# A shared port and measured durations in the cost model of a kernel's planner

## The chip, the cores and the metric

The kernel runs on one core of a Trainium2 chip. The core has five queues of instructions that run side by side: TensorE (PE in the profile; PEld is its weight load), VectorE (DVE), ScalarE (ACT), GpSimd (POOL) and SyncE (SP), which here issues the transfers between HBM and SBUF. Each queue runs in its own order, and semaphores make an instruction wait for instructions of other queues. An instruction that waits holds up everything behind it in its queue. The metric is the time of one execution in microseconds of the device.

## The reference

Two independent layers are computed on inputs of 2048 positions by 1024 channels in fp32, and their results stand side by side in the output of 2048 x 2048.

```python
qkv = (x @ wqkv).reshape(B, S, 3, H, Dh)        # S 2048, D 1024, H 32, Dh 32
scores = jnp.einsum("bhqd,bhkd->bhqk", q, k) * Dh ** -0.5
o = jnp.einsum("bhqk,bhkd->bhqd", softmax(scores), v)
a = o.reshape(B, S, D) @ wo                     # attention, all positions

re = jnp.einsum("bsd,ed->bse", xb, dft_hid_re)
im = jnp.einsum("bsd,ed->bse", xb, dft_hid_im)
b = jnp.einsum("ts,bse->bte", dft_seq_re, re) - jnp.einsum("ts,bse->bte", dft_seq_im, im)
out = jnp.concatenate([a, b], axis=-1)
```

## The kernel before

The dense products (the projection to q, k and v; the two DFTs; the output projection) are done by one level of a seven-product scheme in place of eight block products (`STEPS` and `ORDER` list the seven). Each block product takes a sum or difference of input blocks, and each such operand is split into a high part and a low remainder, both of type fp32r; three matmuls (high by high, low by high, high by low) replace one of full precision. So a 256 KB block, 128 partitions by 512 columns, goes through these steps:

- a load, issued by SP (L380, a second term L389);
- an addition or subtraction of a second block, `raw<-raw,g` (L396), when the scheme asks for it;
- a cast to the high part `h` (L418 on VectorE, L416 on ScalarE when the planner may choose);
- a subtraction for the low part `l` (L421).

L396 and L421, and a few other additions, are instructions with two inputs in SBUF. The planner may give each of them to GpSimd, with a price of `SUB`, or to VectorE, with a price of `ADD`. Tiles with names such as `slot`, `raw`, `er`, `h` and `l` are these operands. Results come out of PSUM by an evacuation on VectorE (L564, L566, L768, L770, L781).

Attention runs per head. Scores S = QK are computed by TensorE into 128 x 1024 tiles of PSUM (L1069), VectorE takes the negative row maximum of each (`negm`, L1075), and ScalarE computes the exponential with row sums (L1078). A second pass computes the scores transposed (T, L1201), with the row maxima as two more rows of the contraction; ScalarE takes their exponential into `pt` (L1205), and TensorE multiplies `pt` with the values in groups of sixteen products (V, L1219). VectorE adds each group to the head's output (L1230, L1232), and the head is scaled by the reciprocal sums (L1247).

The order of the work is not that of the loops. The loops only register operations with the class `Plan`, each with an engine, a cost in microseconds, what it waits for, a rank, and for some a second engine with its own cost and rank. At the end one main loop simulates the machine with these costs. Whenever an engine is free in this simulation, the operation with the lowest rank among those that are able to start is emitted, and its end is computed. TensorE gets the scores, the transposed scores and the value products of the heads in turn, and dense matmuls of the seven-product scheme ("fills") are placed between them at a pace that keeps both streams in proportion. What the simulation decides becomes the fixed order of all five queues. At run time semaphores keep the data right; the times are the machine's own.

The costs stand in `Plan` (`LAT`, `OVERLAP`, `SLACK`, `KB_US`, `LANDING`, `QUEUE`) and in the kernel's body (`MM` for a matmul, `PV` and `SWITCH` for a group of value products, `ES` and `ET` for the two exponentials, `MAX`, `EVAC`, `CAST`, `BIT`, `SUB`, `ADD`). A transfer ends at its place in a bandwidth of `KB_US` KB per us plus `LANDING`; `SLACK` is added before a consumer of a transfer counts as able to start, so that the queues don't run into a transfer that is late. SP may run ahead of the modelled bandwidth by `QUEUE`.

This is the heart of the plan before:

```python
    def start(self, o, e=None):
        e = e or o.engine
        o.emit(e) if o.other else o.emit()
        o.begun = True
        self.free[e] = self.now + (o.cost if e == o.engine else o.other[1])
...
                if not able or self.begin(e) > self.now:
                    break
                self.start(heapq.heappop(able)[3], e)
```

Of the kernel before, what the change touches and what calls it, by code (L numbers as in the profile page):

```python
# [34 lines left out]
class Op:  # L35


    __slots__ = ("engine", "cost", "emit", "rank", "kb", "other", "left", "ready", "end", "begun", "then", "soon", "lanes")

    def __init__(self, engine, cost, emit, rank=0.0, kb=0, other=None):  # L40
        self.engine, self.cost, self.emit, self.rank, self.kb, self.other = engine, cost, emit, rank, kb, other
        self.left, self.ready, self.end, self.begun, self.lanes = 0, -1e3, None, False, 1
        self.then, self.soon = [], []


class Ring:
# [14 lines left out]
class Plan:  # L61
# [22 lines left out]
    def op(self, engine, cost, emit, after=(), uses=(), rank=0.0, kb=0, order=None, other=None, lanes=1):  # L84

        o = Op(engine, cost, emit, rank, kb, other)
        o.lanes = lanes
        seen = set()  # L90
        for d in after:
            if d is not None and id(d) not in seen:
                seen.add(id(d))
                self._wait(o, d)
        for u in uses:
            u.append(o)
        if order is not None:
            p, order.first = order.first, o
            if p is not None and not p.begun:
                p.soon.append(o)  # L100
                o.left += 1
        if o.left == 0:
            self._release(o)
        return o
# [18 lines left out]
    def start(self, o, e=None):  # L123
        e = e or o.engine
        o.emit(e) if o.other else o.emit()
        o.begun = True
        self.free[e] = self.now + (o.cost if e == o.engine else o.other[1])
        if o.kb:
            for _ in range(o.lanes):
                t = max(self.free[e], self.lane[0])  # L130
                self.dma = max(self.dma, t) + o.kb / o.lanes / self.KB_US
                o.end = self.dma + self.LANDING
                self.lane = self.lane[1:] + [o.end]
                if o.lanes > 1:
                    self.free[e] = t + o.cost
        else:
            o.end = self.free[e]
            self.free[e] -= self.OVERLAP.get(e, 0.0)
        for t in o.then:
            t.ready = max(t.ready, self.after(o, e, t))  # L140
            t.left -= 1
            if t.left == 0:
                self._release(t)
        for t in o.soon:
            t.ready = max(t.ready, self.now)
            t.left -= 1
            if t.left == 0:
                self._release(t)
        o.then = o.soon = ()
        o.emit = None  # L150

    def others(self):

        for e, pend in self.pending.items():
            able = self.able[e]
            while True:
                while pend and pend[0][0] <= self.now:
                    t, s, r, o = heapq.heappop(pend)
                    heapq.heappush(able, (r, t, s, o))
                while able and able[0][3].begun:  # L160
                    heapq.heappop(able)
                if not able or self.begin(e) > self.now:
                    break
                self.start(heapq.heappop(able)[3], e)

    def next_time(self):
        t = 1e18
        for e, pend in self.pending.items():
            able = self.able[e]
            while able and able[0][3].begun:  # L170
                heapq.heappop(able)
            while pend and pend[0][3].begun:
                heapq.heappop(pend)
            if able:
                t = min(t, self.begin(e))
            elif pend:
                t = min(t, max(self.begin(e), pend[0][0]))
        return t
# [7 lines left out]
def kernel(  # L186
# [101 lines left out]
    ACAST = 0.6  # L288
# [12 lines left out]
    op = pl.op  # L301
# [56 lines left out]
    def fetch(shape, terms, store=None, keep=None):  # L358

        box = {}  # L360
        raws, seconds, tile_of, gate = where[0]
        rank = seq()
        sign, *first = terms[0]
        loaded = len(first) == 2
        if len(terms) == 1 and not loaded:
            return first[0].get, first[0].made, first[0].users
        if keep is None:
            old, users = raws.take()
        else:
# [12 lines left out]
        for sign, *term in terms[1:]:  # L382
            other = {}
            if len(term) == 2:
                gold, gusers = seconds.take()

                def load(src=term[0], other=other):
                    other["q"] = tile_of(shape, "g", len(seconds.users))
                    nc.sync.dma_start(other["q"], src)  # L389

                q = op("SP", ISSUE, load, gold + term[1] + gate, [gusers], rank, 256, seconds)
            else:
                other["k"], q, gusers = term[0], term[0].made, term[0].users

            def add(e, sign=sign, other=other, a=None if last is not None else first[0]):
                (nc.gpsimd if e == "POOL" else nc.vector).tensor_tensor(  # L396
                    out=dest(), in0=dest() if a is None else a.get(), in1=other["q"] if "q" in other else other["k"].get(), op=ALU.add if sign > 0 else ALU.subtract)

            last = op("POOL", SUB, add, old + [first[0].made if last is None else last, q], [users, gusers] + ([first[0].users] if last is None else []),
                      rank, 0, raws if keep is None and last is None else None, other=("DVE", ADD, 20 + rank))  # L400
            old = []
        if keep is not None:
            keep.made = last
        if store is not None:
            store[1].append(op("SP", ISSUE, lambda: nc.sync.dma_start(store[0], dest()), [last], [users], rank, 256))
        return dest, last, users

    spare = [True]

    def halves(raw, made, users, hi, lo, old, mine, order=(None, None)):  # L410

        rank = seq()
# [7 lines left out]
        def low(e):  # L420
            (nc.gpsimd if e == "POOL" else nc.vector).tensor_tensor(out=lo(), in0=raw(), in1=f(hi()), op=ALU.subtract)  # L421

        a = op("DVE", CAST, high, [made] + old[0], [users, mine[0]], 10 + rank, 0, order[0], ("ACT", ACAST, 25 + rank) if spare[0] else None)
        b = op("POOL", SUB, low, [a] + old[1], [users, mine[0], mine[1]], rank, 0, order[1], other=("DVE", ADD, 25 + rank))
        return a, b

    def piece(terms, store=None):
# [316 lines left out]


    def add_op(emit, after, users, rank):
        return op("POOL", SUB, emit, after, users, rank, other=("DVE", ADD, 20 + rank))

    def gather(what, X, Y, u3, to, wrote, part=None):

# [293 lines left out]
    def scores(h):  # L1044
# [79 lines left out]
    mine = {}  # L1124
    rt = {}

    def sums(h):
# [262 lines left out]
```

## Time and profile before

| what | value |
|---|---|
| median of 3 runs | 3123.39 us (3119.55 to 3124.46) |
| profiled execution, its own time | 3121.61 us |
| profiled execution, span from first to last instruction | 3119.8 us |
| mean granted clock of TensorE | 0.994 |
| TensorE busy | 98% of the span |
| VectorE busy | 80% |
| ScalarE busy | 74% |
| GpSimd busy | 30% |
| moved between HBM and SBUF | 567.77 MB, mean 182 GB/s |

The profile is one execution. A row of a group of instructions names the line, the engine, the operation, what it writes and reads (output <- inputs) and the shapes; then follow the count, the busy time and the mean duration of one in ns, and the idle time of the engine just before them with what ended it. In a timeline a row gives start, duration, engine, line, operation, and in brackets the idle time before it with its releaser. A wait is a triple: total us, times, longest us. Ends of matmuls are modelled, so a matmul's shown duration of about 400 ns overlaps the next one.

### The profile page before, as it was taken

What the parts mean: (1) busy time and instruction counts of PE and PEld (TensorE: products, weight loads), DVE (VectorE), ACT (ScalarE), POOL (GpSimd) and SP (SyncE); (2) the same over time, 40 slices, a digit from 0 to 9 for tenths busy, and PEclk for the clock granted to TensorE, in tenths of its full rate; (3) what the DMA queues carried; (4) which work ended last, traced back from release to release, by engine and by line L of the source; (5) the groups of instructions that cost most, each with busy time, mean ns of one, the idle gap of its engine ahead of it and who ended that gap; (6) DMA issues with size and microseconds to landing.
All of it is one profiled execution on the core that took longest, in us unless ns stands there. A gap on an engine that the chain in (4) does not pass through costs nothing.

```text
span 3119.8 us, 45400 instructions
## 1 busy us (share of the span) xinstructions
PE 3066.8 (98%) x15040; PEld 2151.0 (69%) x15040; DVE 2503.5 (80%) x3182; ACT 2299.1 (74%) x4316; POOL 924.9 (30%) x683
## 2 busy tenths in 40 slices
PE   9899999899999999999999999999999999999999
PEld 7687666566666666666676666666666666666787
DVE  6669888878777878887777798888877888887886
ACT  4237888778888888888888878888888887775321
POOL 3423323412112321122111253323211244433443
PEclk9999999999999999999999999999999999999999
DMA  9975557876634544464433576445433467546952
GB/s 333 326 241 192 184 159 246 291 233 217 182 86 145 190 132 155 135 189 147 133 126 104 180 241 195 146 148 173 141 115 98 141 213 232 159 150 206 330 172 91
DMA packets 359673, 567.77 MB, mean 182 GB/s; under 512 B 86640, under 2 KB 88176, under 8 KB 359440
## 3 DMA queue, kind: packets, MB, share of 16 engines
q1 hardware_dynamic: 359440, 564.87, 56.8%
q8 instruction: 121, 1.98, 0.3%
q14 instruction: 112, 0.92, 0.1%
HBM read 407.70 MB, written 156.50 MB: 181 GB/s over the span
## 4 chain that ended last, share of the span: by engine, by line
PE 66%; DVE 6%; ACT 1%; issue 1%; DMA 0%; POOL 0%; SPq 0%; ACTq 0%; DVEq 0%; POOLq 0%
PE pd L332 29%; PE psT L1201 12%; PE pd L1219 11%; PE psS L1069 11%; PE psT L332 3%; DVE negm L1075 2%; ACT psS L1078 1%; DVE raw L396 1%; DVE h L418 1%; DVE slot L421 1%; DVE l L421 0%; DVE slot L770 0%; DVE slot L418 0%; DVE e L781 0%; PE psS L1152 0%
## 5 line engine op out<-in xcount | busy, mean ns | idle before, releaser
L1075 DVE TENSOR_REDUCE negm<-psS 128x1 f32<-128x1024 f32 x1024 | 1231.9, 1217 | 206.2 <-PE psS L1069 202.4
L1205 ACT ACTIVATE pt<-psT 128x512 f32<-128x512 f32 x2048 | 1155.4, 627 | 322.0 <-PE psT L1201 315.7
L1078 ACT ACTIVATE psS<-psS,negm 128x1024 f32<-128x1024 f32 x1024 | 1146.6, 1120 | 187.0 <-DVE negm L1075 179.9
L332 PE MATMUL pd<-slot,h 128*128 128x512 f32 x3336 | 1157.8, 397 | 3.2 <-DVE ot L1232 1.7
L1201 PE MATMUL psT<-qs,ks 98*128 98x512 f32 x2048 | 822.4, 405 | 5.1 <-ACT pt L1205 4.2
L332 PEld LDWEIGHTS pd<-slot,h 128*128 128x128 f32 x3336 | 632.4, 190 | 156.9 <-issue 12.6
L332 PE MATMUL pd<-slot,l 128*128 128x512 f32 x1668 | 661.5, 397 | 0.8 <-POOL l L421 0.8
L1201 PEld LDWEIGHTS psT<-qs,ks 98*128 98x128 f32 x2048 | 385.9, 189 | 193.2 <-issue 65.6
L1069 PE MATMUL psS<-ks,qs 96*128 96x512 f32 x1552 | 479.0, 399 | 12.1 <-ACT psS L1078 11.1
L1219 PE MATMUL pd<-pt,vt 128*32 128x512 f32 x4096 | 470.9, 601 | 4.5 <-DVE c L564 2.6
L421 POOL TENSOR_TENSOR l<-raw,h 128x512 fp32r<-128x512 f32 x174 | 233.1, 1339 | 798.5 <-DVE h L418 407.7
L396 POOL TENSOR_TENSOR raw<-raw,g 128x512 f32<-128x512 f32 x229 | 307.9, 1348 | 422.6 <-DVE raw L396 102.4
L332 PEld LDWEIGHTS pd<-slot,l 128*128 128x128 f32 x1668 | 316.7, 190 | 76.0 <-issue 5.7
L1069 PEld LDWEIGHTS psS<-ks,qs 96*128 96x128 f32 x1552 | 289.3, 189 | 95.2 <-ACT psS L1078 30.4
L1219 PEld LDWEIGHTS pd<-pt,vt 128*32 128x32 f32 x4096 | 121.2, 110 | 283.6 <-issue 262.1
L421 POOL TENSOR_TENSOR slot<-raw,slot 128x512 fp32r<-128x512 f32 x131 | 182.2, 1396 | 396.6 <-DVE slot L418 319.0
L1078 ACT ACTIVATION_READ_ACCUMULATOR psS<-psS,negm 128x1 f32 x1024 | 242.0, 236 | 0.0
L332 PE MATMUL pd<-slot,slot 128*128 128x512 f32 x768 | 195.9, 393 | 0.0
L1232 DVE TENSOR_TENSOR ot<-ot,pd 128x512 f32<-128x512 f32 x96 | 65.8, 686 | 134.6 <-PE pd L1219 134.5
L332 PEld LDWEIGHTS pd<-slot,slot 128*128 128x128 f32 x768 | 145.0, 189 | 32.2 <-issue 0.4
L418 DVE CAST h<-raw 128x512 fp32r<-128x512 f32 x305 | 153.4, 503 | 15.8 <-PE pd L332 13.8
L421 DVE TENSOR_TENSOR slot<-raw,slot 128x512 fp32r<-128x512 f32 x153 | 156.4, 1025 | 6.0 <-ACT slot L416 2.4
(114 smaller groups left out, 2093.5 us busy)
## 6 DMA issues: line engine op xcount, KB each, us to landing
raw<-in_ct SPq DMA_DIRECT2D x224, 256.0 KB, 3.4
g<-in_ct SPq DMA_DIRECT2D x128, 256.0 KB, 3.5
c<-u_d SPq DMA_DIRECT2D x104, 256.0 KB, 3.6
qk_d<-e SPq DMA_DIRECT2D x52, 512.0 KB, 3.8
qs<-qk_d SPq DMA_DIRECT2D x128, 192.0 KB, 3.7
ks<-qk_d SPq DMA_DIRECT2D x128, 192.0 KB, 2.7
raw<-ab_d SPq DMA_DIRECT2D x96, 256.0 KB, 2.9
g<-ab_d SPq DMA_DIRECT2D x80, 256.0 KB, 3.6
```

The source lines that it names most:

```text
L332: nc.tensor.matmul(box["ps"], a[1]((a[0].hi, a[0].lo)[u]()), b[1]((b[0].hi, b[0].lo)[v]()), start=k == 0, stop=k == n - 1)
L396: (nc.gpsimd if e == "POOL" else nc.vector).tensor_tensor(out=dest(), in0=dest() if a is None else a.get(), in1=other["q"] if "q" in other ...
L418: nc.vector.tensor_copy(hi(), raw())
L421: (nc.gpsimd if e == "POOL" else nc.vector).tensor_tensor(out=lo(), in0=raw(), in1=f(hi()), op=ALU.subtract)
L1069: nc.tensor.matmul(p[:, i * NB : i * NB + NB], (qx["t"] if own else QS[h % 2][0:96])[:, qt * P : qt * P + P], KS[h % 2][0:96, c * 1024 + i ...
L1075: nc.vector.tensor_reduce(out=ST["negm"][:, c, qt : qt + 1], in_=box["p"], axis=AX.X, op=ALU.max, negate=True)
L1078: nc.scalar.activation(box["p"], box["p"], AF.Exp, bias=ST["negm"][:, c, qt : qt + 1], accum_out=ST["sums"][:, c, qt : qt + 1])
L1201: nc.tensor.matmul(box["p"], KS[h % 2][0:98, t * P : t * P + P], QS[h % 2][0:98, j * NB : j * NB + NB], start=True, stop=True)
L1205: nc.scalar.activation(box["t"], box["p"], AF.Exp)
L1219: nc.tensor.matmul(po["p"][j * DH : j * DH + DH, :], VT[h][:, k, :], box["t"], start=(k == t + 1 - PVB), stop=(k == t), tile_position=(0, ...
L1232: nc.vector.tensor_tensor(out=po["o"], in0=po["o"], in1=po["p"], op=ALU.add)
```

## The change

The planner's simulation gets a resource that two engines use. An operation can be marked `two`: a VectorE operation that is taken to use the port that VectorE shares with GpSimd. Marked are the casts (L418), all additions and subtractions that may go to GpSimd or VectorE (L396, L421, L786, L1019, L1247), and the small operations of a head's maxima and sums with inputs in SBUF (L1099, L1137, L1146). Every GpSimd operation counts as a user. While the port is taken in the simulation, GpSimd starts nothing, and VectorE starts the lowest-ranked operation that is not marked, if there is one.

```diff
+        self.port = 0.0
...
         self.free[e] = self.now + (o.cost if e == o.engine else o.other[1])
+        if e == "POOL" or e == "DVE" and o.two:
+            self.port = self.free[e]
...
-                self.start(heapq.heappop(able)[3], e)
+                o = self.choose(e, able)
+                if o is None:
+                    break
+                self.start(o, e)
+
+    def choose(self, e, able):
+        if self.port <= self.now or e not in ("DVE", "POOL"):
+            return heapq.heappop(able)[3]
+        if e == "POOL":
+            return None
+        for x in sorted(able):
+            if not x[3].two and not x[3].begun:
+                able.remove(x)
+                heapq.heapify(able)
+                return x[3]
+        return None
```

The function that finds the next moment of the simulation takes the port into account in the same way. The other part of the change is the numbers. Durations of single operations are replaced, and the model of transfers is changed:

```diff
-    SLACK = {("SP", "POOL"): 2.0, ("SP", "DVE"): 2.5, ("SP", "PE"): 2.0, ("POOL", "DVE"): 0.7}
-    KB_US = 340.0
-    LANDING = 1.8
+    SLACK = {("SP", "POOL"): 2.0, ("SP", "DVE"): 2.0, ("SP", "PE"): 2.0, ("POOL", "DVE"): 0.7}
+    KB_US = 380.0
+    LANDING = 1.6
...
-    MM, PV, SWITCH, TINY = 0.232, 0.87, 0.34, 0.25
-    ES, ET = 1.22, 0.61
-    MAX, EVAC, CAST, BIT = 1.22, 0.69, 0.45, 0.27
-    SUB = 1.34
+    MM, PV, SWITCH, TINY = 0.234, 0.762, 0.62, 0.25
+    ES, ET = 1.235, 0.625
+    MAX, EVAC, CAST, BIT = 1.22, 0.685, 0.415, 0.275
+    SUB = 1.31
...
-    ADD = 0.69
+    ADD = 0.68
...
-        a = op("DVE", BIT, nmin, maxes + nold, [nuse, suse], -2)
+        a = op("DVE", 0.17, nmin, maxes + nold, [nuse, suse], -2, two=True)
...
-        a = op("DVE", 2 * BIT, sub, exps + told, [tuse, suse, nuse], -2)
+        a = op("DVE", 0.24, sub, exps + told, [tuse, suse, nuse], -2, two=True)
...
-        c = op("DVE", 3 * BIT, inv, [b], [tuse, suse], -2)
+        c = op("DVE", 0.67, inv, [b], [tuse, suse], -2, two=True)
```

The set of operations and transfers stays the same. What can change is the order in each of the five queues, and the choice of engine for an operation that has two.

More of the change, by code (lines that the diff above doesn't have):

```diff
@@ L35, with __init__ @@
 class Op:
-    __slots__ = ("engine", "cost", "emit", "rank", "kb", "other", "left", "ready", "end", "begun", "then", "soon", "lanes")
-    def __init__(self, engine, cost, emit, rank=0.0, kb=0, other=None):
+    __slots__ = ("engine", "cost", "emit", "rank", "kb", "other", "left", "ready", "end", "begun", "then", "soon", "lanes", "two")
+    def __init__(self, engine, cost, emit, rank=0.0, kb=0, other=None, two=False):
         self.engine, self.cost, self.emit, self.rank, self.kb, self.other = engine, cost, emit, rank, kb, other
@@ L43, in __init__ @@
         self.then, self.soon = [], []
+        self.two = two
 class Ring:
@@ L80, in __init__, with op @@
         self.dma = 0.0
+        self.port = 0.0
         self.lane = [0.0] * 8
         self.seq = 0
-    def op(self, engine, cost, emit, after=(), uses=(), rank=0.0, kb=0, order=None, other=None, lanes=1):
-        o = Op(engine, cost, emit, rank, kb, other)
+    def op(self, engine, cost, emit, after=(), uses=(), rank=0.0, kb=0, order=None, other=None, lanes=1, two=False):
+        o = Op(engine, cost, emit, rank, kb, other, two)
         o.lanes = lanes
@@ L174, in next_time @@
             if able:
-                t = min(t, self.begin(e))
+                u = self.begin(e)
+                if e == "POOL" or e == "DVE" and all(x[3].two or x[3].begun for x in able):
+                    u = max(u, self.port)
+                    if pend:
+                        u = min(u, max(self.begin(e), pend[0][0]))
+                t = min(t, u)
             elif pend:
@@ L399, in fetch @@
             last = op("POOL", SUB, add, old + [first[0].made if last is None else last, q], [users, gusers] + ([first[0].users] if last is None else []),
-                      rank, 0, raws if keep is None and last is None else None, other=("DVE", ADD, 20 + rank))
+                      rank, 0, raws if keep is None and last is None else None, other=("DVE", ADD, 20 + rank), two=True)
             old = []
@@ L421, in low @@
             (nc.gpsimd if e == "POOL" else nc.vector).tensor_tensor(out=lo(), in0=raw(), in1=f(hi()), op=ALU.subtract)
-        a = op("DVE", CAST, high, [made] + old[0], [users, mine[0]], 10 + rank, 0, order[0], ("ACT", ACAST, 25 + rank) if spare[0] else None)
-        b = op("POOL", SUB, low, [a] + old[1], [users, mine[0], mine[1]], rank, 0, order[1], other=("DVE", ADD, 25 + rank))
+        a = op("DVE", CAST, high, [made] + old[0], [users, mine[0]], 10 + rank, 0, order[0], ("ACT", ACAST, 25 + rank) if spare[0] else None, two=True)
+        b = op("POOL", SUB, low, [a] + old[1], [users, mine[0], mine[1]], rank, 0, order[1], other=("DVE", ADD, 25 + rank), two=True)
         return a, b
@@ L746, in add_op @@
     def add_op(emit, after, users, rank):
-        return op("POOL", SUB, emit, after, users, rank, other=("DVE", ADD, 20 + rank))
+        return op("POOL", SUB, emit, after, users, rank, other=("DVE", ADD, 20 + rank), two=True)
     def gather(what, X, Y, u3, to, wrote, part=None):
```

## The prediction

> **What bounds the kernel now.** I read the busy table first, then the busy times by stage, then the chain of waits, then single stalls in order of time, and last the groups of instructions for the prices. The busy table:
>
> ```profile
> PE 3066.8 (98%) x15040; PEld 2151.0 (69%) x15040; DVE 2503.5 (80%) x3182; ACT 2299.1 (74%) x4316; POOL 924.9 (30%) x683
> ```
>
> TensorE is the bound on average: of 3119.8 us of span it lacks 53 us. A plan that only reorders work can win those 53 us and what the clock loses after them, no more. Where they lie is told by five stages (columns: stretch, its length, then busy time and count of PE, PEld, DVE, ACT, POOL; then granted clock, DMA share, GB/s):
>
> ```profile
> 0.00:156.00 156.00, 138.92 (x575) 112.70 (x576) 103.74 (x130) 57.62 (x96) 60.78 (x48) 0.96 0.98 330
> 156.00:468.00 312.00, 307.87 (x1468) 224.91 (x1470) 255.87 (x332) 216.40 (x398) 94.85 (x70) 1.00 0.61 194
> 468.00:702.00 234.00, 221.34 (x1068) 144.06 (x1061) 194.48 (x258) 177.99 (x335) 71.68 (x54) 0.96 0.79 257
> 702.00:2886.00 2184.00, 2171.39 (x10942) 1485.80 (x10941) 1762.06 (x2239) 1795.06 (x3404) 600.88 (x449) 1.00 0.51 160
> 2886.00:3120.00 234.00, 227.27 (x1000) 183.57 (x998) 187.32 (x226) 52.03 (x85) 96.73 (x63) 0.99 0.58 198
> ```
>
> TensorE's idle time is 17.1 us in the first stage (the DMA engines are full there, 0.98), 4.1 in the second, 12.7 in the third, 12.6 in the fourth and 6.7 in the last. The third stage is the densest after the start, and the clock shows there too: 0.96 over 234 us is 0.08 of it, 19 us, at half speed. One stall of that stage in order of time:
>
> ```profile
> 603.45 3.07 POOL L421 TENSOR_TENSOR slot<-raw,slot 128x512 fp32r<-128x512 f32 x2 [0.36 <-DVE slot L418]
> 603.63 1.78 DVE L421 TENSOR_TENSOR l<-raw,h 128x512 fp32r<-128x512 f32 x1
> 605.33 1.21 DVE L1075 TENSOR_REDUCE negm<-psS 128x1 f32<-128x1024 f32 x1
> 606.63 1.09 ACT L1078 ACTIVATE psS<-psS,negm 128x1024 f32<-128x1024 f32 x1 [2.64 <-DVE negm L1075]
> 608.38 0.50 PE L1201 MATMUL psT<-qs,ks 98*128 98x512 f32 x1 [3.55 <-ACT pt L1205]
> 608.79 0.41 DVE L418 CAST e<-e 128x512 fp32r<-128x512 f32 x1
> 609.24 0.69 DVE L421 TENSOR_TENSOR e<-e 128x512 fp32r<-128x512 f32 x1
> ```
>
> Read it upward from 608.38: TensorE idled 3.55 us for ScalarE's exponential, which had idled 2.64 us for VectorE's maximum, which stood behind a subtraction of 1.78 us. The same operation takes 0.69 us at 609.24. The difference ends with GpSimd's first operation, which had started 0.18 us before it: VectorE waited for GpSimd while holding up its whole queue. The same pattern stands in the fourth stage on the chain of work that ended last (start, duration, what):
>
> ```profile
> 2583.30 1.41 DVE h L418
> 2584.74 1.67 DVE l L421
> 2586.40 1.15 DVE negm L1075
> ```
>
> Over the part of the run that the chain covers (797 us to the end), these lines of VectorE hold 0.5, 0.5, 0.5 and 0.4% of the span, 59 us:
>
> ```profile
> by line: PE pd L332 29.0%; PE psT L1201 11.8%; PE pd L1219 11.1%; PE psS L1069 10.9%; PE psT L332 2.8%; DVE negm L1075 2.2%; ACT psS L1078 0.8%; issue 0.6%; DVE raw L396 0.5%; DVE h L418 0.5%; DVE slot L421 0.5%; DVE l L421 0.4%; DVE slot L
> ```
>
> **The change part by part.** *The port in the plan.* The program runs every queue in the order that the planner wrote, so the planner's false beliefs become real stalls. It believed that a cast takes 0.45 us and a subtraction 0.69 us at any moment. The groups say otherwise (count | busy, mean ns | idle before):
>
> ```profile
> L421 DVE TENSOR_TENSOR slot<-raw,slot 128x512 fp32r<-128x512 f32 x153 | 156.4, 1025 | 6.0 <-ACT slot L416 2.4
> L421 DVE TENSOR_TENSOR l<-raw,h 128x512 fp32r<-128x512 f32 x147 | 117.3, 798 | 5.0 <-ACT h L416 0.7
> L396 DVE TENSOR_TENSOR raw<-raw,g 128x512 f32<-128x512 f32 x143 | 113.1, 799 | 8.0 <-DMA raw<-t_d 2.4 <-POOL raw L396 1.5 <-DMA raw<-in_xb 1.2
> L418 DVE CAST h<-raw 128x512 fp32r<-128x512 f32 x305 | 153.4, 503 | 15.8 <-PE pd L332 13.8 <-POOL l L421 1.2 <-issue 0.3
> L418 DVE CAST slot<-raw 128x512 fp32r<-128x512 f32 x233 | 126.1, 547 | 1.8 <-DMA raw<-ab_d 1.0 <-POOL slot L421 0.2
> ```
>
> Against 0.69 and 0.41 us undisturbed, the excess is 153 x 0.335 + 147 x 0.108 + 143 x 0.109 + 305 x 0.093 + 233 x 0.137 = 51 + 16 + 16 + 28 + 32 = 143 us of VectorE. After the change such an operation is not placed while GpSimd works; a maximum or an evacuation out of PSUM is placed instead, and GpSimd's next operation waits for VectorE's. So 143 us bounds what VectorE can get back, and TensorE sees only what lies on its path. There the 59 us of the chain set the bounds: at the groups' mean (0.33 of a 1025 ns operation is excess, 0.14 of one of 798) 8 to 19 us are excess; if all were like the 1.67 us one, 0.59 of them, 35 us.
>
> *Operations that change engine.* In the built programs GpSimd has 63 tensor operations fewer (688 to 625), VectorE 56 more and ScalarE 7 more; TensorE's 12,928 matmuls (the profile records each attention-value product twice, hence 15,040) and the 2,345 entries of SP's queue keep their number and kinds. VectorE takes on 56 x 0.69 = 39 us; this is covered by the idle 20% of VectorE (616 us) and by the excess that goes. In the third stage VectorE is 194 of 234 us busy and this cover is thin: the longest-loaded part of it has these rows (same columns as the stages):
>
> ```profile
> 536.00:562.00 26.00, 23.27 (x100) 14.99 (x97) 23.03 (x28) 20.14 (x37) 13.99 (x11) 0.87 0.93 323
> 580.00:600.00 20.00, 16.55 (x86) 10.19 (x85) 19.90 (x31) 12.45 (x24) 8.23 (x6) 1.00 0.92 310
> 600.00:612.00 12.00, 8.40 (x38) 4.21 (x40) 9.89 (x13) 7.74 (x14) 4.42 (x3) 0.88 1.00 336
> ```
>
> VectorE is busy without a gap from 580 to 600, with the DMA engines at 0.92. There I expect less to be won than the collisions are worth: what goes first is itself waiting.
>
> *Durations of single operations.* The matmul goes from 0.232 to 0.234, the maximum stays at 1.22, the exponentials become 1.235 and 0.625, a group of sixteen attention-value products goes from 0.34 + 4 x 0.87 = 3.82 to 0.62 + 4 x 0.762 = 3.67 us. A row of the chain agrees with the new value for the group, 3.57 us:
>
> ```profile
> 2512.77 3.57 PE pd L1219 x32
> ```
>
> In the built program the mix is hardly moved: 945 dense matmuls follow the last attention group instead of 953, and 273 precede the first score instead of 281. I price this at nothing for TensorE's work, with 2 us either way for the order in which kinds of matmul follow each other.
>
> *Transfers believed faster and the slack cut.* A 256 KB load for a VectorE operation was taken to be safe 0.46 + 256/340 + 1.8 + 0.1 + 2.5 = 5.6 us after its issue with an idle queue; it becomes 0.46 + 256/380 + 1.6 + 0.1 + 2.0 = 4.8. Here the trace bounds from both sides (median us from issue to landing; the first two from 702 to 2886 us, the next from 540 to 640, the last two from the first 156):
>
> ```profile
> raw<-in_ct SPq DMA_DIRECT2D x206, 256.0 KB, 3.3
> raw<-ab_d SPq DMA_DIRECT2D x96, 256.0 KB, 2.9
> ...
> raw<-in_wqk SPq DMA_DIRECT2D x11, 256.0 KB, 4.9
> ...
> er<-in_xa SPq DMA_DIRECT2D x40, 256.0 KB, 5.3
> raw<-in_xa SPq DMA_DIRECT2D x28, 256.0 KB, 5.6
> ```
>
> In the long fourth stage 4.8 leaves 1.5 us and more of margin, so the cut costs nothing there and may let operands be ready up to 0.8 us earlier. In the third the margin is gone at the median, unless the planner's own queue model, which adds up to 1 us, covers it. What waits behind a late load is all of VectorE's queue, the maxima first, and behind them ScalarE and the scores. I take +3 us for the third stage (two to four waits of about 1 us that reach TensorE), with 0 and 13 as ends, the latter from the rival below. The first stage is bound by bytes at 330 GB/s, which do not change: 0, within 3 either way.
>
> *The sum.* Second stage 4.1 idle: half of it goes, -2. Third stage: 12.7 idle and about 8 more for 19 us at half clock, together some 21; half, -10, plus 3 for late loads. Fourth: 12.6 idle; two thirds, -8, because its loads have margin and VectorE has room. Last stage: about 4 of its 6.7 are the last store, the rest holds one more collision of the same kind: -1.5. First: 0. Together -18.5, and with 1.5 for order -17. The profiled execution took 3121.6 us, so 3104.6; the median of the runs shown is 1.8 higher, so I forecast 3106.
>
> *A rule weighed.* At 603.45 the row shows VectorE's subtraction ending about when GpSimd's operation does, so the port was held for a whole operation. The Trainium skill, SBUF — State Buffer, section "Who interferes with whom", says just that: the pair is locked exclusively for a full instruction, the later one blocks entirely, and which of them suffers is decided by the order of issue alone. The trace agrees (1.78 against 0.69 us). The page therefore speaks against a large gain: a lock that is held can be planned around, but not shortened, and two queues with no semaphore between them still take it in whatever order they arrive. By it the result would be that of the second rival below.
>
> **The rivals.** *Late loads at the head of VectorE's queue (slower).* Place: the stages with full DMA engines. GpSimd absorbed most late loads; VectorE has few such waits (us in sum, times, longest):
>
> ```profile
> POOL l L421 <- DVE h L418: 409.8, 92, 22.7
> ...
> POOL raw L396 <- DMA raw<-in_ct: 49.6, 18, 5.5
> POOL raw L396 <- DMA raw<-in_xb: 47.6, 10, 9.5
> ...
> DVE er L396 <- DMA raw<-in_xa: 12.7, 8, 2.9
> ```
>
> With 0.8 us less slack and more of the adds on VectorE, waits move there. If 80 of the 981 operations of the five groups came 0.8 us late, VectorE would wait 64 us; TensorE lost about 30 us in the middle stages against 143 us of excess, one in five, so +13 us. And a plan whose loads are late no longer keeps GpSimd and VectorE apart, so nothing is won: 3123 + 13 = 3136. It decides when about one in twelve of these operations waits so. For it: 4.9 to 5.6 us to landing in two stages. Against: 3.3 us in the stage that is 70% of the run.
>
> *The order of two queues holds no lock (no change).* The plan only chooses an order for each engine; nothing makes GpSimd start at the planned moment. If the real times drift by more than half of a 1.3 us operation, the collisions fall at other places in like number. For it: landings of equal loads differ between 2.9 and 5.6 us. Against: GpSimd's longest waits in sum end with VectorE's own cast (92 waits above), not with a load, so drift is shared. The gain would be a quarter, 3119.
>
> *All of it goes.* The four middle stages lose two thirds to all of their idle time, the half-clock stretches go with it, and the earlier readiness in the fourth stage adds: 32 idle + 8, less 3: 3086. For it: nearly every stall that I followed in stages two to four has an inflated VectorE operation in front of it. Against: VectorE at 100% from 580 to 600 us.
>
> **How the numbers follow.** Forecast 0.55, its own range 3095 to 3115; no change 0.17; slower 0.14; all of it 0.14. Outside 0.2% (6 us, about what a measurement of this kernel can tell) lie the forecast almost whole and the third rival: faster 0.69. Within: the second rival and a little of the forecast, 0.18. Slower: the first, 0.13. The range reaches to 3088, which leaves out most of the third rival's lower half, and to 3130, which leaves out most of the first; together no more than 2 in 10.
>
> **What the new profile would show.** Right: the means of the five groups above fall towards 690 and 415 ns (1025 to under 850, 547 to under 480); VectorE's lines L396, L418, L421 hold under 1.3% of the chain, not 1.9; TensorE's idle time falls from 53 to about 38 us, most in 468 to 702 and 702 to 2886, with a clock of 0.98 or more in the third stage; the first stage stays at 17. Wrong by the first rival: new waits of VectorE for loads, above 30 us in sum. Wrong by the second: means unchanged. What I could have missed is a change of the work's order that starves ScalarE of scores; it would show as idle TensorE in the fourth stage before the scores, with the groups' means down all the same.

## The result

The changed kernel takes 3089.56 us (median of 4 runs, 3087.53 to 3091.51) against 3122.46 us before (4 runs); the ratio is 0.9895, with a 95% interval of 0.9878 to 0.9912. That is 33 us less; the forecast was 17 us less, 3106 with a range down to 3088. The profiled execution took 3091.5 us with a span of 3089.7.

The busy table of the changed kernel (its code lines have numbers higher by 25, so L396, L418, L421, L1075 and L1078 are now L421, L443, L446, L1100 and L1103):

```profile
PE 3052.6 (99%) x15040; PEld 2154.2 (70%) x15040; DVE 2432.0 (79%) x3238; ACT 2312.0 (75%) x4323; POOL 828.8 (27%) x620
```

TensorE's idle time fell from 53.0 to 37.1 us, and its busy time fell too, by 14.2 us, with the same 15,040 records. To see where, the two executions have to be cut at the same amount of TensorE's work. First the changed kernel, cut where the start of its 575th, 2043rd, 3111th and 14,053rd record lies (columns as in the prediction: stretch, length, PE, PEld, DVE, ACT, POOL, clock, DMA share, GB/s):

```profile
0.00:157.30 157.30, 139.84 (x575) 112.05 (x576) 103.76 (x145) 60.01 (x98) 41.78 (x35) 0.95 0.98 338
157.30:467.60 310.30, 308.46 (x1470) 227.58 (x1468) 245.01 (x331) 216.30 (x397) 95.70 (x72) 1.00 0.61 192
467.60:688.70 221.10, 215.62 (x1071) 143.50 (x1070) 185.78 (x251) 179.70 (x339) 80.13 (x60) 0.98 0.82 270
688.70:2862.20 2173.50, 2165.34 (x10943) 1490.93 (x10942) 1720.38 (x2275) 1803.14 (x3402) 549.12 (x412) 1.00 0.51 161
2862.20:3089.70 227.50, 223.28 (x989) 180.16 (x987) 177.06 (x240) 52.88 (x91) 62.08 (x41) 1.00 0.57 198
```

Then the kernel before, cut at the same records:

```profile
0.00:155.90 155.90, 138.82 (x574) 112.64 (x575) 103.64 (x130) 57.62 (x96) 60.78 (x48) 0.96 0.98 330
155.90:468.40 312.50, 308.37 (x1472) 225.07 (x1475) 256.37 (x333) 216.80 (x399) 94.85 (x70) 1.00 0.61 194
468.40:704.10 235.70, 223.04 (x1073) 145.66 (x1066) 196.18 (x259) 179.48 (x337) 72.39 (x54) 0.96 0.80 257
704.10:2888.50 2184.40, 2171.78 (x10943) 1486.16 (x10942) 1760.65 (x2239) 1793.78 (x3402) 600.18 (x448) 1.00 0.51 160
2888.50:3119.80 231.30, 224.77 (x989) 181.50 (x987) 186.63 (x225) 51.44 (x84) 96.73 (x63) 0.99 0.58 197
```

The same work takes +1.4, -2.2, -14.6, -10.9 and -3.8 us, in sum the 30.1 us by which the spans differ. In this pair of plans nearly half comes from the third stage, in which VectorE and the DMA engines are both densely loaded. The nudged kernels below show that this stage moves by up to 12 us with any new order, and that the fourth stage gains in every pair.

The groups of VectorE that the prediction used, in the changed kernel (count | busy, mean ns | idle before):

```profile
L443 DVE CAST h<-raw 128x512 fp32r<-128x512 f32 x305 | 138.6, 455 | 20.0 <-PE pd L357 17.0 <-DMA raw<-in_xb 1.1 <-issue 1.0
L446 DVE TENSOR_TENSOR l<-raw,h 128x512 fp32r<-128x512 f32 x176 | 131.8, 751 | 5.8 <-ACT h L441 2.1
L443 DVE CAST slot<-raw 128x512 fp32r<-128x512 f32 x230 | 115.0, 504 | 3.9 <-DMA raw<-in_wd 3.2
L421 DVE TENSOR_TENSOR raw<-raw,g 128x512 f32<-128x512 f32 x148 | 114.7, 783 | 8.4 <-DMA raw<-t_d 3.0 <-DMA raw<-in_ct 1.5 <-DMA g<-ab_d 1.1
L446 DVE TENSOR_TENSOR slot<-raw,slot 128x512 fp32r<-128x512 f32 x142 | 105.4, 747 | 5.5 <-ACT slot L441 3.1
```

With the prediction's undisturbed durations (0.69 and 0.41 us) the excess is 305 x 0.045 + 176 x 0.061 + 230 x 0.094 + 148 x 0.093 + 142 x 0.057 = 14 + 11 + 22 + 14 + 8 = 69 us, where it was 143. By this measure half of the collisions' cost is gone, not all.

One wait of ScalarE stands between such a collision and TensorE: the exponential of a score tile that waits for its maximum (total us, times, longest). Before:

```profile
ACT psS L1078 <- DVE negm L1075: 179.9, 167, 8.3
```

After:

```profile
ACT psS L1103 <- DVE negm L1100: 111.9, 122, 8.7
```

This wait fell with the time here, but it does not set the time alone: one kernel below (transfers alone) has 148.6 us of it and the time of before, another (without GpSimd) has 110.1 us and is 16 us slower than the changed one. The chain of waits in the fourth stage moved as well. Before (the chain reaches back to 796 us), maxima held 3.2% of the time and the casts, additions and subtractions another 2.6%:

```profile
by line: PE pd L332 36.8%; PE psT L1201 16.9%; PE pd L1219 15.7%; PE psS L1069 15.6%; DVE negm L1075 3.2%; ACT psS L1078 1.2%; DVE h L418 0.8%; issue 0.7%; DVE l L421 0.6%; DVE slot L418 0.4%; DVE slot L421 0.4%; DVE raw L396 0.4%; PE psS L
```

After, maxima hold half of that share, and of the others only `h` and `raw` stand in the part of the line that is shown:

```profile
by line: PE pd L357 40.2%; PE psT L1226 18.5%; PE pd L1244 17.4%; PE psS L1094 16.9%; DVE negm L1100 1.6%; ACT psS L1103 0.6%; issue 0.6%; PE psS L1177 0.4%; PE psS L1128 0.4%; DVE h L443 0.4%; DVE raw L421 0.3%; DMA g<-ab_d 0.3%; POOL raw 
```

### The profile page after: what moved, and what is told of

Same layout as the page of the kernel before. It is cut to its first block, busy times and chain, and to the rows that moved or that the text cites. A ratio compares the mean times of both kernels' runs of the same rounds, so it can differ in the third digit from the quotient of the medians.

```text
span 3089.7 us, 45419 instructions
## 1 busy us (share of the span) xinstructions
PE 3052.6 (99%) x15040; PEld 2154.2 (70%) x15040; DVE 2432.0 (79%) x3238; ACT 2312.0 (75%) x4323; POOL 828.8 (27%) x620
## 4 chain that ended last, share of the span: by engine, by line
PE 90%; DVE 4%; DMA 4%; issue 1%; ACT 1%; SPq 1%; POOL 0%; POOLq 0%; ACTq 0%; DVEq 0%
PE pd L357 39%; PE psT L1226 15%; PE psS L1094 15%; PE pd L1244 15%; PE psT L357 6%; DVE negm L1100 1%; DMA er<-in_xa 1%; ACT psS L1103 1%; DMA raw<-in_wqk 0%; DMA raw<-in_wv 0%; DMA qk_d<-e 0%; DVE raw L421 0%; DMA raw<-in_xa 0%; DVE h L443 0%; PE psS L1177 0%
## 5 line engine op out<-in xcount | busy, mean ns | idle before, releaser
L1100 DVE TENSOR_REDUCE negm<-psS 128x1 f32<-128x1024 f32 x1024 | 1234.8, 1220 | 224.6 <-PE psS L1094 220.0
L1103 ACT ACTIVATE psS<-psS,negm 128x1024 f32<-128x1024 f32 x1024 | 1139.5, 1113 | 122.2 <-DVE negm L1100 111.9
L446 POOL TENSOR_TENSOR l<-raw,h 128x512 fp32r<-128x512 f32 x145 | 194.3, 1340 | 876.5 <-DVE h L443 374.0
L421 POOL TENSOR_TENSOR raw<-raw,g 128x512 f32<-128x512 f32 x224 | 294.7, 1322 | 483.9 <-DVE raw L421 75.6
L446 POOL TENSOR_TENSOR slot<-raw,slot 128x512 fp32r<-128x512 f32 x142 | 198.8, 1405 | 492.8 <-DVE slot L443 334.4
L1103 ACT ACTIVATION_READ_ACCUMULATOR psS<-psS,negm 128x1 f32 x1024 | 234.5, 229 | 0.0
L443 DVE CAST h<-raw 128x512 fp32r<-128x512 f32 x305 | 138.6, 455 | 20.0 <-PE pd L357 17.0
L1094 PE MATMUL psS<-ks,qx 96*128 96x512 f32 x496 | 151.2, 397 | 1.7 <-ACT psS L1103 1.4
```

The lines of the kernel that those rows point to most:

```text
L443: nc.vector.tensor_copy(hi(), raw())
L1094: nc.tensor.matmul(p[:, i * NB : i * NB + NB], (qx["t"] if own else QS[h % 2][0:96])[:, qt * P : qt * P + P], KS[h % 2][0:96, c * 1024 + i ...
L1100: nc.vector.tensor_reduce(out=ST["negm"][:, c, qt : qt + 1], in_=box["p"], axis=AX.X, op=ALU.max, negate=True)
L1103: nc.scalar.activation(box["p"], box["p"], AF.Exp, bias=ST["negm"][:, c, qt : qt + 1], accum_out=ST["sums"][:, c, qt : qt + 1])
```

## The experiments

The change has three parts: the port in the plan, the durations, the transfer numbers. My theory was that the port carries the gain. The rivals were the corrected numbers, and the luck of a new order: a planner like this turns any small change into another order of five queues.

**The port alone, and the numbers alone.** The first kernel is the changed one with the numbers of before, the second the kernel before with all numbers of the change.

```diff
 # port alone: the changed kernel, and
-    SLACK = {..., ("SP", "DVE"): 2.0, ...};  KB_US = 380.0;  LANDING = 1.6
+    SLACK = {..., ("SP", "DVE"): 2.5, ...};  KB_US = 340.0;  LANDING = 1.8
-    MM, PV, SWITCH, TINY = 0.234, 0.762, 0.62, 0.25
+    MM, PV, SWITCH, TINY = 0.232, 0.87, 0.34, 0.25
 # and so on for every duration; numbers alone is the reverse, on the kernel before
```

> The port in the plan, with every duration and transfer number of before. My theory (the gain of 33 us comes from keeping VectorE's two-port operations and GpSimd apart): most of it, 3095 to 3107 us, the groups slot<-raw,slot and l<-raw,h at 700 to 800 ns on VectorE as in the changed kernel. Rival (the corrected durations and transfer numbers carry it): 3112 to 3124. Rival (any new order of the plan moves the time as much): anything from 3080 to 3140.

> All the numbers of the change (durations and transfers), without the port. My theory: 3110 to 3122 us, the means of the VectorE groups unchanged from before (1025, 798, 799, 503, 547 ns). Rival (the numbers carry it): 3089 to 3100.

The port alone: 3086.67 us, ratio 0.9886 (0.9872 to 0.9901). The numbers alone: 3143.14 us, ratio 1.0067 (1.0051 to 1.0082). So the port carries the whole gain, more than I expected of it, and the numbers without it make the kernel slower by 20.5 us, which neither expectation had foreseen. The stages of the kernel with the numbers alone, cut at the same records, show where:

```profile
151.40:473.10 321.70, 313.36 (x1471) 226.21 (x1473) 266.89 (x342) 218.92 (x401) 90.48 (x66) 0.99 0.60 189
473.10:701.50 228.40, 217.51 (x1071) 141.97 (x1072) 199.02 (x263) 181.20 (x343) 64.34 (x48) 0.99 0.81 262
701.50:2899.70 2198.20, 2176.48 (x10944) 1484.90 (x10943) 1793.99 (x2297) 1802.74 (x3396) 529.71 (x392) 1.00 0.51 159
2899.70:3142.80 243.10, 229.44 (x989) 183.02 (x987) 186.11 (x225) 50.73 (x83) 93.69 (x61) 0.98 0.54 185
```

Against the kernel before, +9 us in the second stage, -7 in the third, +14 in the fourth and +12 in the last. Its collisions are as many as before (two of the five groups):

```profile
L421 DVE TENSOR_TENSOR l<-raw,h 128x512 fp32r<-128x512 f32 x184 | 155.1, 843 | 9.8 <-ACT h L416 4.8
L421 DVE TENSOR_TENSOR slot<-raw,slot 128x512 fp32r<-128x512 f32 x151 | 150.9, 1004 | 6.9 <-ACT slot L416 3.2
```

The excess of these two is 184 x 0.153 + 151 x 0.314 = 76 us, against 67 for the same two before. Corrected durations of undisturbed operations don't tell a plan of collisions.

**Is it the luck of an order?** `LATE` is a margin that TensorE's operations get in the plan; it stands for nothing that was measured. Moved by 3%, it gives all queues a new order.

```diff
-    LATE = 0.3
+    LATE = 0.31
```

> The kernel before with one constant of the planner that stands for nothing measured moved by 3% (LATE from 0.30 to 0.31), which gives the queues a new order. My theory: within 6 us of before, 3117 to 3128. Rival (any new order moves the time as much as the change did): more than 12 us away.

> The changed kernel with the same constant moved by 3% (LATE from 0.30 to 0.31). My theory: within 6 us of the changed kernel, 3084 to 3096. Rival (the 33 us are the luck of one order): closer to the kernel before than to the changed one, above 3105.

> The port with the numbers of before, and LATE at 0.31. The nudge moved the kernel before by 10 us and the changed kernel by 13, so a single pair tells no more than some 12 us. If the port carries the gain in any order: 3082 to 3105, at least 20 us under the nudged kernel before (3133). If port_alone was the luck of one order: above 3110.

> The numbers without the port, and LATE at 0.31. If the numbers without the port truly cost 20 us: 3135 to 3150. If the 3143 of the first try were the spread of orders: 3115 to 3135. Either way at least 20 us above the nudged changed kernel (3103), if the port carries the gain.

Medians in us, with the ratio to the kernel before in brackets where it was not given yet:

| | no port, LATE 0.30 | no port, LATE 0.31 | port, LATE 0.30 | port, LATE 0.31 |
|---|---|---|---|---|
| numbers of before | 3122.46 | 3132.87 (1.0023 to 1.0046) | 3086.67 | 3096.93 (0.9907 to 0.9937) |
| numbers of the change | 3143.14 | 3162.81 (1.0119 to 1.0149) | 3089.56 | 3102.66 (0.9923 to 0.9953) |

I had expected the nudge to stay within 6 us; it costs 10 to 20 us in each of the four pairs, so a difference of that size between two single plans tells nothing of its cause. The nudged kernel with the new numbers alone lies above both ranges that I had set for it. The port is outside of that spread: -36, -36, -54 and -60 us in the four pairs. The new numbers cost 21 and 30 us without the port, and 3 and 6 us with it, which is inside the spread. So in these plans the numbers did harm only to a planner that didn't know the port.

The same traces tell which stage the port shortens. Lengths in us, cut at the same records as above:

| | no port, LATE 0.30 | no port, LATE 0.31 | port, LATE 0.30 | port, LATE 0.31 |
|---|---|---|---|---|
| third stage, numbers of before | 235.7 | 245.5 | 221.9 | 233.8 |
| third stage, numbers of the change | 228.4 | 237.0 | 221.1 | 223.7 |
| fourth stage, numbers of before | 2184.4 | 2184.0 | 2172.6 | 2162.9 |
| fourth stage, numbers of the change | 2198.2 | 2208.8 | 2173.5 | 2179.1 |

The rows of the fourth stage in the four nudged kernels, in the order before, port alone, numbers alone, changed:

```profile
717.80:2901.80 2184.00, 2171.78 (x10947) 1486.04 (x10943) 1766.92 (x2267) 1795.05 (x3388) 575.80 (x431) 1.00 0.51 161
699.70:2862.60 2162.90, 2162.37 (x10950) 1493.03 (x10942) 1706.73 (x2271) 1790.33 (x3384) 571.23 (x423) 1.00 0.52 162
707.00:2915.80 2208.80, 2182.28 (x10950) 1494.25 (x10946) 1792.75 (x2296) 1799.59 (x3388) 555.08 (x409) 1.00 0.52 159
686.20:2865.30 2179.10, 2169.39 (x10944) 1495.41 (x10943) 1750.07 (x2312) 1794.41 (x3388) 535.53 (x398) 1.00 0.52 162
```

In the fourth stage every plan with the port is shorter than every plan without it, by 12 to 30 us in the pairs. In the third the pairs give 7 to 14 us, but the nudge alone moves it by 3 to 12, and the two kinds of plan overlap.

**Which of the numbers.**

```diff
 # transfers alone, on the kernel before
-    SLACK = {..., ("SP", "DVE"): 2.5, ...};  KB_US = 340.0;  LANDING = 1.8
+    SLACK = {..., ("SP", "DVE"): 2.0, ...};  KB_US = 380.0;  LANDING = 1.6
 # durations alone, on the kernel before
-    MAX, EVAC, CAST, BIT = 1.22, 0.69, 0.45, 0.27
+    MAX, EVAC, CAST, BIT = 1.22, 0.685, 0.415, 0.275
 # and all other durations of the change
```

> The kernel before with the three transfer numbers alone (KB_US 380, LANDING 1.6, slack of VectorE behind a load 2.0). If the late loads of my first rival cost what the numbers alone lost (20 us): 3135 to 3150, with VectorE's waits for loads above 40 us. If the durations cost it: 3115 to 3133, within what a nudge of the plan does.

> The kernel before with the corrected durations alone. If they cost what the numbers alone lost (a shorter belief of a cast and a subtraction packs VectorE's port work closer, so that collisions grow): 3133 to 3150, the groups slot<-raw,slot and raw<-raw,g above 1000 and 840 ns. If the transfers cost it: 3110 to 3133.

Transfers alone: 3119.83 us, ratio 0.9997 (0.9988 to 1.0007). Durations alone: 3129.17 us, ratio 1.0028 (1.0019 to 1.0037). With the transfers alone VectorE's waits for loads do rise, from 24 us to 52 us, which is the sign that I had named, but the time stays; so late loads are not what the numbers lost. The wait for the maxima is shorter than before, without a gain:

```profile
ACT psS L1078 <- DVE negm L1075: 148.6, 140, 6.2
```

The durations cost 9 us, as much as a nudge does, and of the two means that I had named one grew past its mark (1041 ns) and the other didn't (828 ns). The two parts together lost 20.5 us. The 11 us between that and the sum of the parts are of the size of a nudge, and what caused them stays open.

**What of the port brings it.** In the changed plan two things happen while GpSimd holds the port: VectorE's marked operations wait, and others go first. This kernel was meant to keep the first and take the second away (the function that finds the next moment is changed to match):

```diff
-        for x in sorted(able):
-            if not x[3].two and not x[3].begun:
-                able.remove(x)
-                heapq.heapify(able)
-                return x[3]
-        return None
+        return None if able[0][3].two else heapq.heappop(able)[3]
```

> The changed kernel, but while the port is taken VectorE waits with its first-ranked operation in the plan instead of letting an unmarked one go first. Theory A (the gain comes from the maxima and evacuations that go first): most of the gain is gone, 3108 to 3125. Theory B (the gain comes from a plan that knows how long VectorE really takes): it stays, 3086 to 3100. In both the groups' means stay at 740 to 790 ns.

3112.05 us, ratio 0.9968 (0.9956 to 0.9979): 22 us of the 33 are gone, in the range of theory A. The collisions are about as rare as in the changed kernel:

```profile
L438 DVE CAST h<-raw 128x512 fp32r<-128x512 f32 x305 | 143.8, 472 | 23.4 <-PE pd L352 17.8 <-DMA raw<-in_ct 1.9 <-DMA r_d<-rs 1.3
L441 DVE TENSOR_TENSOR slot<-raw,slot 128x512 fp32r<-128x512 f32 x149 | 111.3, 755 | 8.2 <-ACT slot L436 5.4
```

and the exponentials wait longer for the maxima, 139.9 us against 111.9:

```profile
ACT psS L1098 <- DVE negm L1095: 139.9, 147, 8.0
```

But the edit takes away less than theory A needs, so it can't decide between the two. In both kernels the planner starts the lowest rank first, and maxima and evacuations have the ranks 0 and -1, while casts, additions and subtractions have 10 and more. So a maximum that becomes able to start while GpSimd holds the port goes ahead of a waiting cast in this kernel too. What the edit takes away is the overtaking of a head's small marked operations (L1099, L1137 and L1146 before), which have rank -2. In the plan of the changed kernel an unmarked operation overtakes a marked one 31 times, each time one of these and never a cast, an addition or a subtraction.

So this run prices something narrower: the small operations hold up VectorE's queue in the plan while they wait for GpSimd. It cost 22 us on one pair of plans, where the nudge moves the kernels with the port by 10 and 13. Of the 22 us, 11.5 lie in the third stage (232.6 against 221.1), the one that moves with any new order; the fourth takes 2178.2 us, still within the four plans with the port above. Whether the port's gain comes from the maxima that go ahead or from a plan that knows how long VectorE takes stays open: no run gives VectorE true durations without letting the maxima pass.

**No GpSimd at all.** The change also takes 63 operations off GpSimd. This kernel takes off all of them:

```diff
-            heapq.heappush(self.pending[o.engine], (o.ready, self.seq, o.rank, o))
+            if o.engine != "POOL":
+                heapq.heappush(self.pending[o.engine], (o.ready, self.seq, o.rank, o))
```

> The changed kernel, but no addition or subtraction goes to GpSimd: all 620 run on VectorE at 0.69 us, so no collision is left. VectorE would be busy 2432 + 620 x 0.69 less about 70 of excess, 2790 us or 90%. My theory (GpSimd is worth having, if it is kept apart): 3100 to 3140. Rival (what the change won is only the work taken off GpSimd): at most 3090. The five groups' means fall to 690 and 410 to 420 ns in both.

3105.24 us, ratio 0.9949 (0.9934 to 0.9964). GpSimd keeps 8 small operations of 4.3 us, the collisions are gone, and VectorE has the clean durations on which the sums above rest:

```profile
PE 3065.5 (99%) x15040; PEld 2160.8 (70%) x15040; DVE 2658.4 (86%) x3856; ACT 2306.9 (74%) x4317; POOL 4.3 (0%) x8
...
L447 DVE TENSOR_TENSOR slot<-raw,slot 128x512 fp32r<-128x512 f32 x284 | 192.0, 686 | 4.6 <-ACT slot L442 3.2
L444 DVE CAST slot<-raw 128x512 fp32r<-128x512 f32 x233 | 96.5, 420 | 4.6 <-DMA raw<-ab_d 2.6 <-DMA raw<-in_wv 1.0 <-DMA raw<-in_xa 0.2
```

That is 16 us under the kernel before, which is inside what a nudge can move. The closer comparison has the same numbers in its plan: the kernel with the numbers alone takes 3143.14 us, 38 us more, and the same with the nudge 58 more. (The port is still in this kernel's plan. There it acts on VectorE alone, which passes its own marked operations in the 0.08 us by which the plan lets two of VectorE's operations overlap.) So with these numbers and a plan that was blind to the port, GpSimd's work cost more than it gave; with the numbers of before this is not shown. Against the changed kernel the stages are these (cut at the same records, the third to the last):

```profile
463.30:703.70 240.40, 226.82 (x1072) 145.23 (x1065) 216.08 (x321) 187.97 (x354) 0.00 (x0) 0.96 0.77 248
703.70:2876.20 2172.50, 2167.79 (x10944) 1495.55 (x10943) 1888.73 (x2687) 1790.66 (x3382) 0.00 (x0) 1.00 0.51 162
2876.20:3104.00 227.80, 223.16 (x989) 180.25 (x987) 170.83 (x283) 52.34 (x88) 0.00 (x0) 1.00 0.56 198
```

The third stage, where VectorE is now 90% busy, is longer than in each of the four plans with the port (240.4 us against 221.1 to 233.8); the fourth is within their spread (2172.5 against 2162.9 to 2179.1). The whole is 16 us slower than the changed kernel, but only 3 us slower than the changed kernel with the nudge, so what a GpSimd kept apart is worth is shown for the third stage at most. I had expected VectorE at 2790 us and it has 2658: the durations of its records add up to 2894 us (2584 in the changed kernel), but neighbouring records overlap, and the busy time counts an overlap once.

**Can the rest be had?** Two attempts on the port alone: hold the port 0.15 us longer in the plan, and let GpSimd start nothing while a marked operation of VectorE's own, which is a cast or a small one of a head, is ready (the function that finds the next moment is changed to match).

```diff
-            self.port = self.free[e]
+            self.port = self.free[e] + 0.15
 # and, in the other kernel
-                o = self.choose(e, able)
+                o = None if e == "POOL" and self.cast_able() else self.choose(e, able)
+    def cast_able(self):
+        return any(x[3].two and x[3].engine == "DVE" and not x[3].begun for x in self.able["DVE"])
```

> The port with the numbers of before, but each user holds it 0.15 us longer in the plan. About 70 us of excess are left in the five groups of the changed kernel. If they come from starts that drift by a tenth or two from the plan: the means fall to 720 and 460 ns or less, and the time to 3075 to 3087. If the drift is larger than that (loads that land at other times): means as in port_alone, 3083 to 3100.

> The port with the numbers of before, and in the plan GpSimd starts nothing while a cast of VectorE is ready to start, so that no cast waits for GpSimd's 1.3 us in the plan; GpSimd keeps about 430 tensor operations. If casts held up by GpSimd are what is left of the loss: 3070 to 3085. If VectorE's time is what is short, as in the kernel without GpSimd: 3090 to 3108.

The margin: 3089.45 us, ratio 0.9900 (0.9883 to 0.9916). Casts first: 3095.48 us, ratio 0.9916 (0.9901 to 0.9931); GpSimd kept 530 tensor operations there, not about 430, and the time lies in the range that I had set for VectorE's time being what is short, which is no proof within the nudge's spread. Neither beats the port alone. With the margin two of the five means reached the marks of 720 and 460 ns (`l` 720, `h` 457), and the others didn't fall, two of them here (519 and 806 ns, where the port alone has 521 and 758):

```profile
PE 3053.9 (99%) x15040; PEld 2158.7 (70%) x15040; DVE 2394.5 (78%) x3163; ACT 2300.4 (74%) x4320; POOL 935.8 (30%) x698
...
L443 DVE CAST slot<-raw 128x512 fp32r<-128x512 f32 x229 | 117.8, 519 | 3.4 <-PE psT L357 1.6 <-DMA raw<-o_d 0.6 <-POOL raw L421 0.4
L446 DVE TENSOR_TENSOR slot<-raw,slot 128x512 fp32r<-128x512 f32 x116 | 92.5, 806 | 4.0 <-ACT slot L441 2.3
```

So most of the collisions that are left are not starts that miss the plan by a tenth or two. The first line settles another point: GpSimd is busy for 935.8 us here, as long as before the change, and the kernel is still 33 us faster. So the gain does not need work to be taken off GpSimd.

## Why the prediction was right, and where its sizes were off

- *The sign and the mechanism were right as far as they were tested.* The port gives -36 to -60 us in four pairs of plans, and with it the means of the five groups and VectorE's share of the chain fell. Which part of the port does it, the maxima that pass or the true time of VectorE in the plan, is not shown.
- *The hit on the range is in part luck.* 3089.56 lies 1.6 us inside the lower end, 3088; the port alone, at 3086.67, lies outside, and the nudged changed kernel, at 3102.66, is close to the forecast. One plan of this kind can't tell whether -17 or -33 is nearer; the four pairs say that -17 was too little.
- *A row was misread.* The subtraction at 603.63 doesn't end "about when GpSimd's operation does": the row of 3.07 us holds two operations of GpSimd, and the subtraction ends at 605.41, inside the second. Taken apart, the first ends at 604.86. A clean subtraction of 0.69 us that ends at 605.41 would have started at 604.72, so the reading that the prediction gave first, that VectorE waited for GpSimd's first operation, fits to 0.14 us. A smaller slip: of the 2,112 records beyond the 12,928 matmuls, 2,048 are attention-value products, and the other 64 belong to the two small products of a head (L1103, L1152).
- *The means.* 1025 ns was to fall under 850 and came to 747; 547 was to fall under 480 and came to 504, a miss. Half of the 143 us of excess went (to 69). The four entries of the chain that held 1.9% of the span (`raw`, `h`, `slot` and `l`) hold 1.1%, under the 1.3% that was named.
- *TensorE's idle time* was to be 38 us and is 37.1, with the first stage about as before (17.5 after 17.1) and the third stage's clock at 0.98 as said.
- *The size was half of what came.* In the sum, the third stage was sized at 7 us (10 of its 21, less 3 for late loads) and gave 14.6; the fourth at 8 and gave 10.9; the last at 1.5 and gave 3.8; the 1.5 for order was not there. The third stage's miss is no larger than what a nudge does to it. The fourth stage is the term that was too small in every pair of plans: 12 to 30 us in the four above. There I had counted two thirds of TensorE's idle time alone, and TensorE's busy time for the same 10,943 records fell as well, by 6.4 us (2171.8 to 2165.3), with a granted clock of 1.00 in both. Since ends of matmuls are modelled, busy time can hold short waits; what the 6.4 us were is not shown.
- *What goes first is itself waiting* (the reason for halving the third stage). In the changed kernel the records that took 20.0 us around 580 to 600 take 17.0, and VectorE is busy for 14.6 of them, so there it didn't hold. In the nudged port alone they take 21.5 with VectorE busy for 20.9. How full VectorE is there hangs on the plan.
- *Late loads* (first rival). VectorE's waits for loads did rise, from 24 us in 23 waits to 46 us in 47, above the 30 us that I had named as the sign. Yet the transfer numbers alone brought 52 us of such waits and cost nothing (0.9997), so the step from such a wait to TensorE, one in five, was wrong for them.
- *No lock between two queues* (second rival). It would explain the half of the collisions that is left, and the margin of 0.15 us that changed little fits; no run shows it. It did not decide the time: half of the excess went all the same, where it had all of it stay. So the rule that the prediction weighed was no reason against a gain.
- *All of it goes* (third rival, 3086) was nearest in time but not in mechanism: 37 us of idle time and 69 us of excess are still there.
- *Durations priced at nothing.* With the port that holds (3 and 6 us, inside the spread of nudges). Without the port the same numbers cost 21 and 30 us; the prediction had no such interaction.

## What to carry to other kernels

If two engines lock each other out, tell the planner of it; here that was worth 36 to 60 us, and new numbers without that knowledge made the kernel slower in both pairs. Price a stall by what stands behind it in its queue: here a subtraction that took 1 us longer held up a maximum, an exponential and TensorE. Before a few us are put down to a cause in a kernel whose order comes out of a planner, move a meaningless constant by 3%: here that alone was worth 10 to 20 us. And before a run is taken to leave out one half of a mechanism, count how often the plan uses what the edit removes: here the clause that lets operations pass was used 31 times, and the ranks did the rest.

## What was not expected of the hardware

An engine that helps can cost more than it gives: with the same numbers in the plan, and on one plan each, GpSimd's work placed without regard to VectorE made the kernel 38 us slower than leaving GpSimd idle. And in 70% of the run (the fourth stage) GpSimd made no difference beyond the spread of plans even when it was kept apart, 2162.9 to 2179.1 us with it and 2172.5 without. Small operations of VectorE pay as well: the minimum `tt<-nm,negm` of 128 x 16 on VectorE takes 301 ns before and 157 ns with GpSimd idle.
